# A kernel of window attention and an MLP: the first attention block of a batch moved to the period ahead, loads and casts re-ordered, closing stores on two queues

## The chip, the cores and the metric

The kernel runs on one core of one Trainium2 chip. A core has a matrix engine (TensorE, PE in the profile, its weight loads PEld), a vector engine (VectorE, DVE), a scalar engine (ScalarE, ACT), a general engine (GpSimd, POOL) and a synchronisation engine (SyncE, SP) that here only issues DMAs. Every engine works through its own instruction stream in order and meets the others through semaphores. SBUF is the working memory of 128 partitions, PSUM the memory into which TensorE writes. The metric is the device time of one execution in microseconds. A profile shows one such execution; its span runs from the first to the last instruction.

## The reference

For 8 batches, 8 heads, 576 positions and head width 64, the kernel computes attention in which position i sees the 64 positions i-63 to i, lays the heads side by side (512 columns), and runs a normalised two-layer MLP with a residual:

```python
scores = (1.0 / np.sqrt(D)) * np.matmul(q, k.transpose(0, 1, 3, 2))
mask = (rel >= 0) & (rel < 64)                  # rel = i - j
attn = softmax(np.where(mask, scores, -1e9))
x = np.matmul(attn, v).transpose(0, 2, 1, 3).reshape(B, S, H * D)

xn = (x - mean(x)) / np.sqrt(var(x) + 1e-06) * g_ln
out = x + np.maximum(xn @ w_ch1, 0.0) @ w_ch2   # 512 -> 2048 -> 512
```

All inputs and the output are float32 in HBM; the kernel multiplies in float16 and accumulates in float32.

## The kernel before

**Groups.** The MLP runs on nine groups of 512 rows. Groups 0 to 7 are the first 512 positions of each batch; group 8 gathers the last 64 positions of all eight batches (the tails). A group's rows fall into four blocks of 128 rows. A block of a batch is two windows of 64 queries; a block of group 8 holds the tails of two batches.

**Attention of a block** is cut into steps. `s_mm` forms the scores of a block (16 matmuls L263 into two PSUM tiles `sc`, of which there are two in all) and their exponentials (two ACT operations, L266) into a tile `pt`; `s_mask` multiplies by the mask on DVE (L273). `b_step` multiplies by the values (16 matmuls L291 into `xps`, one PSUM tile in all), divides by the row sums (L294, L297) into the float32 rows `xn`, and takes mean and variance (L299, L302). `z_step` normalises a row block on POOL in four operations (L316 to L319). `zt_step` transposes it on PE (L328), and ACT copies it into `zT` (L331), the input of the MLP.

**Inputs.** `load_qk` and `load_v` fetch a batch's q, k and v from HBM (SP, L92 and L139). The float32 buffers are two per tensor for the halves of q and k and one for v, so a load waits until POOL has cast what was there: `cast_qk` (L126), `cast_v` (L145). `t_main` transposes a half of q or k on PE (L216), and ACT or DVE copies it into `qkT`. Values are kept twice: `vA`, and `vB`, which is `vA` shifted by 64 rows. `make_vB` makes the shift with two DMAs issued by POOL (L163, L164). Tails have the same steps: `load_tail`, `cast_tail` and `t_tail`; their loads use the buffers of q and k.

**MLP of a group.** Sixteen units `l1` (four matmuls of 512 columns, L363, and a ReLU on ACT, L367) are followed, from group 2 on, by fourteen units `stage`: the second layer as seven products of half-sized blocks (L435, eight matmuls of 256 columns a unit), in the order 1, 2, 6, 5, 7, 4, 3, two units each. The sums that these products take as operands come from DVE: `s_sums` (L414) of the hidden values, `w2_sums` (L532) of the weights, once. `post` adds a product into `xn` on DVE (L442); products 1, 6 and 7 share one PSUM tile (`pA`), so product 6 waits for the add of product 1. `store` writes finished rows out (SP, L401); for group 8 `store_rest` does (L395). Groups 0 and 1 have a plain second layer (L375, L499).

**The order of work is written out by hand.** Period g runs the units of group g. After unit i come the steps put into slot i by calls `at(i, step, ...)`; within a slot they run in the order in which the calls were made, and each step appends its instructions to the engines' streams. From period 2 on a period has 30 units (numbers 0 to 29, the first 16 of them `l1`). A slot fixes an order only: a DMA on SP is issued as soon as the ones queued ahead of it are issued and its buffer is free. In period g the attention of batch g+1 is computed and batch g+2 is loaded, cast and transposed. From period 2 on the four blocks of batch g+1 have `s_mm` in slots 1, 5, 10, 15, `b_step` and `z_step` in 6, 11, 16, 21 and `zt_step` in 12, 17, 22, 27. A table places the tail blocks:

```python
TAILS = {3: [0], 5: [1], 7: [2, 3]}
```

The rows `xn` of a batch lie in two buffers of 256 rows out of four, so the rows of batch g+1 overwrite those of batch g-1, once these are stored. The stores of a period are issued after products 4 and 3, which are its last.

## Time and profile before

| What | Value |
|---|---|
| median of 13 runs | 334.2 us (332.93 to 337.15) |
| time of the profiled execution | 335.8 us |
| its span | 334.1 us |
| granted TensorE clock, mean | 0.993 |
| PE busy | 315.2 us, 94% |
| DVE busy | 202.6 us, 61% |
| ACT busy | 174.6 us, 52% |
| POOL busy | 165.0 us, 49% |
| HBM read and written | 38.80 and 9.44 MB |

Times in the profile are microseconds, unless marked ns. A row of a timeline gives the start, the length, the engine, the line and operation, output and inputs, how many instructions were merged, and in brackets how long the engine stood idle before it and what ended that wait. A row of waits gives who waited for what, then the total, the number of times and the longest. A row of busy time by stretch gives the length of the stretch and, for each engine, its busy time and its instructions, then the granted clock (1.00 is full), the share of DMA and its GB/s. Periods 2, 3, 4, 5, 6, 7 and 8 begin at about 98.0, 134.8, 170.9, 203.7, 239.8, 271.2 and 301.9 us. Matmuls overlap in the pipeline, so a busy time of several is longer than the step from one group to the next.

### The profile page before, as it was taken

To read this page: it belongs to the slowest core of one execution; us is meant where nothing else is said; L and a number is where in the kernel's file an instruction comes from. 1 tells how busy PE (TensorE), PEld (TensorE's weight loads), DVE (VectorE), ACT (ScalarE), POOL (GpSimd) and SP (SyncE) were. 2 spreads that over 40 slices of the span, in tenths; PEclk is the share of its full clock that TensorE was granted. 3 is DMA by queue.
4 is the path that set the end of the run, shared out by engine and by line. 5 is a ranking of instruction groups with operands and counts; after the bars stand their busy time and mean duration, and the time that the engine had idled before them with its cause. 6 is when DMAs were issued, how large, how long until landed. Compare 5 with 4: busy or idle time off the path is not lost.

```text
span 334.1 us, 7795 instructions
## 1 busy us (share of the span) xinstructions
PE 315.2 (94%) x3229; PEld 203.9 (61%) x3229; DVE 202.6 (61%) x388; ACT 174.6 (52%) x292; POOL 165.0 (49%) x251
## 2 busy tenths in 40 slices
PE   7998999999996999999899999998999999999992
PEld 4566445786543478546764686466745874685582
DVE  0796583676852796179645964599448744671542
ACT  2486515485356562785357636863477137605600
POOL 7588656503990397448743776377616342420000
PEclk9999999999999899999999999999999999999999
DMA  8999999956129826892059586940391048003013
GB/s 193 290 382 278 343 273 330 264 177 121 65 78 244 191 48 97 238 266 59 3 153 317 108 143 171 301 90 3 76 241 25 0 151 134 2 2 126 0 33 96
DMA packets 85638, 51.08 MB, mean 153 GB/s; under 512 B 55681, under 2 KB 76673, under 8 KB 85602
## 3 DMA queue, kind: packets, MB, share of 16 engines
q1 hardware_dynamic: 84672, 47.98, 53.5%
q0 software_dynamic: 640, 2.33, 3.7%
q8 instruction: 25, 0.41, 0.5%
q10 hardware_dynamic: 290, 0.26, 0.2%
q14 instruction: 11, 0.09, 0.1%
HBM read 38.80 MB, written 9.44 MB: 144 GB/s over the span
## 4 chain that ended last, share of the span: by engine, by line
PE 61%; DMA 11%; DVE 11%; POOL 9%; SPq 3%; issue 3%; ACT 1%; POOLq 0%; ACTq 0%
PE hps L363 22%; PE pA L435 9%; PE pC L435 7%; PE pB L435 6%; PE hph L484 4%; DMA qk<-in_q_dram 4%; DMA w2s<-in_moe_w_ch_dram 3%; DVE sS L414 3%; PE ch L375 3%; PE xps L291 3%; DMA vB<-vA 3%; PE tp L216 3%; PE sc L263 2%; DVE stats L299 2%; DVE xn L297 2%
## 5 line engine op out<-in xcount | busy, mean ns | idle before, releaser
L363 PE MATMUL hps<-zT,w1g 128*128 128x512 f16 x480 | 113.8, 382 | 0.7 <-ACT zT L331 0.7
L367 ACT ACTIVATE hrT<-hps 128x512 f16<-128x512 f32 x120 | 71.9, 601 | 36.9 <-PE hps L363 36.0
L363 PEld LDWEIGHTS <-w1g 128*128 128x128 f16 x480 | 44.0, 98 | 48.7 <-issue 3.5
L316 POOL TENSOR_SCALAR rsz<-mvg 128x1 f32<-128x1 f32 x28 | 12.5, 448 | 90.8 <-DVE mvg L302 90.2
L331 ACT COPY zT<-ztp 128x512 f16<-128x512 f16 x36 | 21.0, 584 | 56.8 <-PE ztp L328 56.7
L435 PEld LDWEIGHTS <-sS 128*128 128x128 f16 x448 | 42.6, 98 | 7.8 <-issue 3.0
L266 ACT ACTIVATE pt<-sc 128x512 f16<-128x512 f32 x72 | 39.0, 597 | 10.5 <-PE sc L263 10.3
L207 ACT COPY qkT<-tp 128x1024 f16<-128x1024 f16 x26 | 26.2, 1012 | 26.5 <-PE tp L216 26.2
L126 POOL CAST qk<-qk 128x1024 f16<-128x1024 f32 x32 | 34.3, 1090 | 8.5 <-DMA qk<-in_q_dram 4.2
L435 PEld LDWEIGHTS <-hrT 128*128 128x128 f16 x336 | 31.7, 98 | 4.1
L273 DVE TENSOR_TENSOR pt<-pt,mask 128x1024 f16<-128x1024 f16 x28 | 19.1, 682 | 23.6 <-ACT pt L266 23.6
L414 DVE TENSOR_TENSOR sS<-hrT 128x512 f16<-128x512 f16 (+1 forms) x42 | 24.7, 588 | 11.1 <-ACT hrT L367 11.1
L442 DVE TENSOR_TENSOR xn<-pA,xn 128x512 f32<-128x512 f32 x28 | 19.2, 685 | 19.0 <-PE pA L435 11.2
L294 DVE RECIPROCAL rcp<-xps 128x8 f32<-128x8 f32 x36 | 7.3, 203 | 38.3 <-PE xps L291 38.1
L435 PE MATMUL pA<-wT,sS 128*128 128x256 f16 x224 | 27.6, 273 | 2.5 <-DVE xn L442 2.5
L435 PE MATMUL pC<-w2s,sS 128*128 128x256 f16 x224 | 27.6, 273 | 0.0
L299 DVE BATCH_NORM_STATS2 stats<-xn 128x6 f32<-128x512 f32 x36 | 25.0, 695 | 1.2
L297 DVE TENSOR_TENSOR xn<-xps,rcp 128x512 f32<-128x512 f32 x36 | 24.9, 691 | 1.2
L319 POOL TENSOR_SCALAR z<-xn,rsz 128x512 f16<-128x512 f32 x28 | 23.9, 852 | 2.9
L484 PE MATMUL hph<-zT,w1g 128*128 128x256 f16 x192 | 23.2, 273 | 1.8 <-ACT zT L331 0.9
L375 PE MATMUL ch<-w2s,hrT 128*128 128x512 f16 x96 | 23.9, 380 | 0.1
L291 PEld LDWEIGHTS <-pt 128*64 128x64 f16 x576 | 12.4, 111 | 15.1 <-issue 10.7
(85 smaller groups left out, 442.4 us busy)
## 6 DMA issues: line engine op xcount, KB each, us to landing
out_dram<-xn SPq DMA_DIRECT2D x34, 256.0 KB, 3.8
qk<-in_q_dram SPq DMA_DIRECT2D x16, 512.0 KB, 7.1
qk<-in_k_dram SPq DMA_DIRECT2D x16, 512.0 KB, 7.7
v<-in_v_dram SPq DMA_DIRECT2D x32, 256.0 KB, 6.1
w2s<-in_moe_w_ch_dram SPq DMA_DIRECT2D x12, 512.0 KB, 5.9
w1s<-in_moe_w_ch_dram SPq DMA_DIRECT2D x4, 512.0 KB, 6.6
tk<-in_k_dram SPq DMA_DIRECT2D x8, 256.0 KB, 4.5
tv<-in_v_dram SPq DMA_DIRECT2D x8, 256.0 KB, 4.7
```

What stands on the lines that cost most here:

```text
L126: nc.gpsimd.tensor_copy(out=dst[:, :].rearrange("p (a j) e d -> p a e j d", j=j), in_=t[:, :].rearrange("p (a e j d) -> p a e j d", e=2, j ...
L207: nc.scalar.copy(out=out, in_=in_)
L266: nc.scalar.activation(out=pt[:, par], in_=sc[par], func=AF.Exp, bias=0.0, scale=scale)
L297: nc.vector.tensor_tensor(out=xn, in0=xps[:, :, 0:D], in1=rcp_b, op=ALU.mult)
L299: nc.vector.bn_stats(out=stats, in_=xv)
L319: nc.gpsimd.tensor_scalar(out=z, in0=xv, scalar1=rs, scalar2=nm, op0=ALU.mult, op1=ALU.add)
L363: nc.tensor.matmul(out=hps, lhsT=w1g[:, kc, 128 * hc:128 * (hc + 1)], rhs=zT[g][:, kc, :], start=(kc == 0), stop=(kc == NKC - 1),)
L367: nc.scalar.activation(out=hrT[:, hc, :], in_=hps, func=AF.Relu, bias=0.0, scale=1.0)
L375: nc.tensor.matmul(out=ch[kb], lhsT=hrT[:, hc, 128 * kb:128 * (kb + 1)], rhs=w2s[:, hc, :], start=(hc == 0), stop=(hc == NHC - 1),)
L414: nc.vector.tensor_tensor(out=o, in0=x, in1=y, op=op)
L435: nc.tensor.matmul(out=bank[which][:, p, :], lhsT=a[:, c, 128 * p:128 * p + 128], rhs=wv[:, c, :], start=(first and p == 0 and c == 0), st ...
L484: nc.tensor.matmul(out=hps[:, e], lhsT=w1g[:, kc, 128 * hc:128 * (hc + 1)], rhs=zT[g][:, kc, 256 * half:256 * half + 256], start=(kc == 0) ...
```

## The change

- Block 0 of a batch has its `s_mm` and `s_mask` in the period ahead (slots 27 and 28; slot 31 in period 1). Blocks 1 to 3 have `s_mm` in 2, 7, 12; `b_step` and `z_step` of all four are in 2, 7, 12, 17, and `zt_step` in 8, 13, 18, 23.
- `load_qk` and `load_v` of batch g+3 are placed in period g, in slots 17, 18 and 23, behind the casts of batch g+2; in period 1 those of batch 4 are added to those of batch 3.
- `cast_qk` of the first half is put ahead of the `b_step` and `z_step` of slot 12 (slot 11, and called earlier than they are), the second in slot 16; `cast_v` and `make_vB` in 20 and 21; `t_main` in 17, 19, 21, 25. In period 1 the same steps come earlier by some six slots.
- Tails have float32 buffers of their own for k and v. Their loads are in slot 5 and their casts in slot 24 of the period ahead, the transpositions (`t_tail`, split in q and k) in 27 and 29; `s_mm` is in slot 1, `b_step` in 5, `zt_step` in 11. The second tail of period 7 is loaded from slot 25 of period 6, cast in slot 3 and transposed in 7 and 8 of period 7, with `s_mm` in 10, `b_step` in 14 and `zt_step` in 20.
- The last two stores go one to SP's queue and one to ACT's, instead of both to ACT's.
- `pt` has four buffers instead of six, and a constant is cut from 128 elements to 1.

```diff
@@ -46,7 +46,7 @@
     p_in = ctx.enter_context(tc.tile_pool(name="pin", bufs=2))
     p_qkt = ctx.enter_context(tc.tile_pool(name="pqkt", bufs=2))
     p_va = ctx.enter_context(tc.tile_pool(name="pva", bufs=2))
-    p_pt = ctx.enter_context(tc.tile_pool(name="ppt", bufs=6))
+    p_pt = ctx.enter_context(tc.tile_pool(name="ppt", bufs=4))
     p_xn = ctx.enter_context(tc.tile_pool(name="pxn", bufs=4))
     p_blk = ctx.enter_context(tc.tile_pool(name="pblk", bufs=3))
     p_grp = ctx.enter_context(tc.tile_pool(name="pgrp", bufs=2))
@@ -96,8 +96,8 @@
 
     def load_tail(i):
         tq = p_in.tile([128, H, D], FP32, tag="tq32", name=f"tq32_{i}", bufs=1)
-        tk = p_in.tile([128, 2, H, D], FP32, tag="qk32_1", name=f"tk32_{i}")
-        tv = p_in.tile([128, 2, H, D], FP32, tag="qk32_0", name=f"tv32_{i}")
+        tk = p_in.tile([128, 2, H, D], FP32, tag="tk32", name=f"tk32_{i}", bufs=1)
+        tv = p_in.tile([128, 2, H, D], FP32, tag="tv32", name=f"tv32_{i}", bufs=1)
         tail32[i] = (tq, tk, tv)
         for r in range(2):
             b = 2 * i + r
@@ -222,20 +222,20 @@
         evac(x if eng is None else eng, dst.rearrange("c h (p j) -> c h p j", j=j),
              tp[:, :].rearrange("c (h j) p -> c h p j", j=j))
 
-    def t_tail(i):
-        q16, k16 = tail16.pop(i)
-        tqk = (p_qkt.tile([128, NHP, 128], FP16, tag="tqT", name=f"tqT_{i}", bufs=1),
-               p_qkt.tile([128, 2, NHP, 128], FP16, tag="tkT", name=f"tkT_{i}", bufs=1))
-        tailT[i] = tqk
-        tp = t_tile([128, 2, NHP, 128], f"tpk_{i}")
-        for r in range(2):
+    def t_tail(i, x):
+        src = tail16[i][x]
+        if x == 0:
+            tailT[i] = (p_qkt.tile([128, NHP, 128], FP16, tag="tqT", name=f"tqT_{i}", bufs=1),
+                        p_qkt.tile([128, 2, NHP, 128], FP16, tag="tkT", name=f"tkT_{i}", bufs=1))
+            tp = t_tile([128, NHP, 128], f"tpq_{i}")
             for hp in range(NHP):
-                nc.tensor.transpose(out=tp[:, r, hp, :], in_=k16[:, r, 2 * hp:2 * hp + 2, :], identity=ident16)
-        evac(0, tqk[1], tp)
-        tp = t_tile([128, NHP, 128], f"tpq_{i}")
-        for hp in range(NHP):
-            nc.tensor.transpose(out=tp[:, hp, :], in_=q16[:, 2 * hp:2 * hp + 2, :], identity=ident16)
-        evac(0, tqk[0], tp)
+                nc.tensor.transpose(out=tp[:, hp, :], in_=src[:, 2 * hp:2 * hp + 2, :], identity=ident16)
+        else:
+            tp = t_tile([128, 2, NHP, 128], f"tpk_{i}")
+            for r in range(2):
+                for hp in range(NHP):
+                    nc.tensor.transpose(out=tp[:, r, hp, :], in_=src[:, r, 2 * hp:2 * hp + 2, :], identity=ident16)
+        evac(0, tailT[i][x], tp)
 
     def s_mm(g, j, pe_mask=False):
         sc = [ps_s.tile([128, NHP, 2, 64], FP32, tag="sc", name=f"sc_{g}_{j}_{par}") for par in range(2)]
@@ -392,7 +392,7 @@
         def store_rest(k0, cols, eng):
             xv = x_norm[(g, k0 // 2)]
             for r in range(2):
-                eng.dma_start(
+                (eng or (nc.sync, nc.scalar)[r]).dma_start(
                     out=out[2 * k0 + r:2 * k0 + r + 3:2, SM:S, cols].rearrange("k s d -> s k d"),
                     in_=xv[64 * r:64 * r + 64, :, cols],
                 )
@@ -471,7 +471,7 @@
                 tbank["shared"] = False
                 tbank["n"] = 0
                 if last:
-                    store_rest(0, slice(256, DM), nc.scalar)
+                    store_rest(0, slice(256, DM), None)
                 else:
                     store(0)
                     store(1)
@@ -535,7 +535,7 @@
     load_qk(0, 0)
     load_v(0, 0, 2)
     g1 = p_const.tile([1, DM], FP32, tag="g1", name="g1")
-    ones1 = p_const.tile([1, 128], FP32, tag="ones1", name="ones1")
+    ones1 = p_const.tile([1, 1], FP32, tag="ones1", name="ones1")
     nc.scalar.dma_start(out=g1, in_=bass.AP(tensor=moe_g_ln.tensor, offset=moe_g_ln.offset, ap=[[DM, 1], [1, DM]]))
     load_qk(0, 1)
     load_v(0, 2, 4)
@@ -691,45 +691,66 @@
                 at(22 + 3 * m, w2_sums, i, 0, 4)
                 at(23 + 3 * m, w2_sums, i, 4, 8)
             for j in range(4):
-                at((9, 13, 16, 20)[j], s_mm, 2, j)
-                at((10, 14, 17, 21)[j], s_mask, 2, j)
-                at((13, 17, 21, 25)[j], b_step, 2, j)
-                at((13, 17, 21, 25)[j], z_step, 2, j)
-                at((19, 23, 27, 31)[j], zt_step, 2, j)
-        if g > 1 and b < B:
-            for j in range(4):
-                at((1, 5, 10, 15)[j], s_mm, b, j)
-                at((2, 6, 11, 16)[j], s_mask, b, j)
-                at((6, 11, 16, 21)[j], b_step, b, j)
-                at((6, 11, 16, 21)[j], z_step, b, j)
-                at((12, 17, 22, 27)[j], zt_step, b, j)
-        for n, i in enumerate(TAILS.get(g, ())):
-            ts = ((3, 5, 6, 9, 15), (14, 16, 17, 20, 26))[n] if g == B - 1 else (3, 8, 9, 13, 19)
-            at(ts[0], t_tail, i)
-            at(ts[1], s_mm, NGRP - 1, i)
-            at(ts[2], s_mask, NGRP - 1, i)
-            at(ts[3], b_step, NGRP - 1, i)
-            at(ts[3], z_step, NGRP - 1, i)
-            at(ts[4], zt_step, NGRP - 1, i)
+                at((9, 13, 16, 19)[j], s_mm, 2, j)
+                at((10, 14, 17, 20)[j], s_mask, 2, j)
+                at((13, 17, 20, 23)[j], b_step, 2, j)
+                at((13, 17, 20, 23)[j], z_step, 2, j)
+                at((19, 23, 26, 30)[j], zt_step, 2, j)
+            at(8, load_qk, 3, 0)
+            at(9, load_qk, 3, 1)
+            at(14, load_v, 3, 0, 4)
+            at(13, alloc_qkT, 3)
+            at(13, cast_qk, 3, 0)
+            at(17, cast_qk, 3, 1)
+            at(21, alloc_v, 3)
+            at(21, cast_v, 3, 0, 2)
+            at(22, cast_v, 3, 2, 4)
+            at(22, alloc_vB, 3)
+            at(22, make_vB, 3)
+            at(31, s_mm, 3, 0)
+            at(31, s_mask, 3, 0)
+            for i, (x, half) in zip((21, 24, 25, 28), ((0, 0), (1, 0), (0, 1), (1, 1))):
+                at(i, t_main, 3, x, half, 0)
+            at(25, load_qk, 4, 0)
+            at(26, load_qk, 4, 1)
+            at(28, load_v, 4, 0, 4)
         if g == 2:
             at(3, w2_sums, 1, 0, 4)
             at(4, w2_sums, 1, 4, 8)
-        if 0 < g and b + 1 < B:
-            n = b + 1
-            e = 20 if g == 1 else 13
-            at(max(e - 12, 2), load_qk, n, 0)
-            at(max(e - 11, 3), load_qk, n, 1)
-            at(e - 6, load_v, n, 0, 4)
-            at(e if g == 1 else e - 1, alloc_qkT, n)
-            at(e if g == 1 else e - 1, cast_qk, n, 0)
-            at(e + 4 if g == 1 else e + 5, cast_qk, n, 1)
-            at(e + 7 if g == 1 else 22, alloc_v, n)
-            at(e + 7 if g == 1 else 22, cast_v, n, 0, 2)
-            at(e + 8 if g == 1 else 23, cast_v, n, 2, 4)
-            at(e + 8 if g == 1 else 23, alloc_vB, n)
-            at(e + 8 if g == 1 else 23, make_vB, n)
-            for (x, half), i in zip(((0, 0), (1, 0), (0, 1), (1, 1)), (24, 26, 28, 30) if g == 1 else (17, 19, 24, 29)):
+        if g > 1 and g + 2 < B:
+            at(11, alloc_qkT, g + 2)
+            at(11, cast_qk, g + 2, 0)
+        if g > 1 and b < B:
+            for j in range(4):
+                if j:
+                    at((2, 7, 12)[j - 1], s_mm, b, j)
+                    at((3, 8, 13)[j - 1], s_mask, b, j)
+                at((2, 7, 12, 17)[j], b_step, b, j)
+                at((2, 7, 12, 17)[j], z_step, b, j)
+                at((8, 13, 18, 23)[j], zt_step, b, j)
+        for n, i in enumerate(TAILS.get(g, ())):
+            ts = (10, 11, 14, 20) if n else (1, 2, 5, 11)
+            at(ts[0], s_mm, NGRP - 1, i)
+            at(ts[1], s_mask, NGRP - 1, i)
+            at(ts[2], b_step, NGRP - 1, i)
+            at(ts[2], z_step, NGRP - 1, i)
+            at(ts[3], zt_step, NGRP - 1, i)
+        n = g + 2
+        if g > 1 and n < B:
+            at(16, cast_qk, n, 1)
+            at(20, alloc_v, n)
+            at(20, cast_v, n, 0, 2)
+            at(21, cast_v, n, 2, 4)
+            at(21, alloc_vB, n)
+            at(21, make_vB, n)
+            for i, (x, half) in zip((17, 19, 21, 25), ((0, 0), (1, 0), (0, 1), (1, 1))):
                 at(i, t_main, n, x, half, 0)
+            at(27, s_mm, n, 0)
+            at(28, s_mask, n, 0)
+            if n + 1 < B:
+                at(17, load_qk, n + 1, 0)
+                at(18, load_qk, n + 1, 1)
+                at(23, load_v, n + 1, 0, 4)
         if g > 1:
             for i in range(1, 5):
                 at(7 + i, s_sums, 0, 4, i)
@@ -737,11 +758,16 @@
                 at((15, 15, 19, 21)[i - 1], s_sums, 6, 8, i)
         for n, i in enumerate(TAILS.get(g + 1, ())):
             if n == 0:
-                at(21, load_tail, i)
-                at(26, cast_tail, i)
+                at(5, load_tail, i)
+                at(24, cast_tail, i)
+                at(27, t_tail, i, 0)
+                at(29, t_tail, i, 1)
+            else:
+                at(25, load_tail, i)
         if len(TAILS.get(g, ())) == 2:
-            at(0, load_tail, TAILS[g][1])
-            at(8, cast_tail, TAILS[g][1])
+            at(3, cast_tail, TAILS[g][1])
+            at(7, t_tail, TAILS[g][1], 0)
+            at(8, t_tail, TAILS[g][1], 1)
         for i, u in enumerate(units):
             if g > 1 and i == 20:
                 tbank["shared"] = True
```

## The prediction

> **What bounds the kernel now.** I read the page first, then busy time by period, then who waited for whom on PE, and last the timelines around each wait.
>
> ```profile
> span 334.1 us, 7795 instructions
> ...
> PE 315.2 (94%) x3229; PEld 203.9 (61%) x3229; DVE 202.6 (61%) x388; ACT 174.6 (52%) x292; POOL 165.0 (49%) x251
> ```
>
> PE works 94% of the span and no other engine more than 61%. The change takes no matrix work away, so only PE's gaps can be won. Busy time cut at the first matmul of periods g = 2, 3 and 4 (stretch, its length, busy us and instructions of each engine, clock, DMA):
>
> ```profile
> core 0: us, PE busy (x) PEld busy (x) DVE busy (x) ACT busy (x) POOL busy (x), PEclk, DMA share, GB/s
> ...
> 98.00:134.80 36.80, 34.06 (x352) 22.18 (x352) 21.57 (x42) 18.41 (x31) 20.84 (x33) 0.95 0.66 144
> 134.80:170.90 36.10, 34.62 (x404) 23.06 (x401) 24.29 (x46) 21.81 (x37) 22.66 (x34) 1.00 0.48 131
> 170.90:203.70 32.80, 32.73 (x355) 21.73 (x353) 20.71 (x41) 19.32 (x32) 18.38 (x29) 1.00 0.76 184
> ```
>
> Period 4 is what an undisturbed period looks like: 32.8 us, PE busy for 32.73. Period 2 has almost the same matmuls (352 against 355) and takes 4.0 us more, part of it at a lower clock. Period 3, with a tail block, has 1.5 us of PE idle. The waits of PE over the whole run (us in total, times, longest):
>
> ```profile
> PE xps L291 <- DMA vB<-vA: 2.6, 1, 2.6
> PE pA L435 <- DVE xn L442: 2.5, 3, 1.1
> ...
> PE ztp L328 <- POOL z L319: 1.3, 3, 0.6
> ```
>
> With one of 0.67 below, these are all the larger ones after the prologue, and all lie at places that the change rearranges: 7.1 us. The prologue's waits are left alone.
>
> **Period 1 into 2.** The PE timeline there:
>
> ```profile
> 96.97 0.39 PE L328 MATMUL ztp<-ident,z 128*128 128x128 f16 x4
> 98.03 1.89 PE L363 MATMUL hps<-zT,w1g 128*128 128x512 f16 x8 [0.67 <-ACT zT L331]
> ...
> 100.19 3.77 PE L363 MATMUL hps<-zT,w1g 128*128 128x512 f16 x16
> ...
> 107.90 0.23 PE L291 MATMUL xps<-vB,pt 128*64 128x65 f16 x1 [2.64 <-DMA vB<-vA]
> ...
> 108.49 4.67 PE L363 MATMUL hps<-zT,w1g 128*128 128x512 f16 x16
> ```
>
> The last transposition of batch 2 ends the period, and the next layer needs its copy at once: 0.67. Then block 0 of batch 3 waits 2.64 for the shifted values, and the 16 matmuls behind it take 4.67 where 3.77 is usual: 0.90 lost to the clock. Each break costs a little beyond its idle time, because matmuls overlap. The size of that comes from a break in period 6 (timeline), beside the same 16 matmuls unbroken on the chain of waits:
>
> ```profile
> 259.20 1.91 PE L435 MATMUL pB<-w2s,hrT 128*128 128x256 f16 x16
> 261.43 1.80 PE L435 MATMUL pA<-wT,sS 128*128 128x256 f16 x15 [0.32 <-DVE xn L442]
> ```
> ```profile
> 166.90 1.75 PE pB L435 x16
> ```
>
> The step is 2.23 where 1.75 is usual: 0.48, of which 0.32 is shown as idle, so 0.16 a break. The boundary loses 0.67 + 2.64 + 2 x 0.16 + 0.90 = 4.5 us.
>
> After the change block 0's scores go to period 1's end (slot 31), its values are wanted at slot 2 instead of 6, and the shift of V is issued at slot 22 instead of 28. What sets the issue is POOL's queue:
>
> ```profile
> 85.42 0.32 POOL L203 MEMSET qkT<- 128x256 f16 x1
> 85.68 2.02 POOL L126 CAST qk<-qk 128x1024 f16<-128x1024 f32 x2
> ...
> 90.26 1.09 POOL L319 TENSOR_SCALAR z<-xn,rsz 128x512 f16<-128x512 f32 x1
> ...
> 93.40 0.51 POOL L316 TENSOR_SCALAR rsz<-mvg 128x1 f32<-128x1 f32 x1
> ...
> 95.87 0.76 POOL L319 TENSOR_SCALAR z<-xn,rsz 128x512 f16<-128x512 f32 x1
> ...
> 99.08 0.74 POOL L163 DMA_DIRECT2D vB<-vA  x1
> 99.83 0.54 POOL L164 DMA_DIRECT2D vB<-vA  x1
> ```
>
> From 85.42 to 100.37 POOL has no gap worth the name. The first half's cast (0.3 + 2.0) moves ahead into an earlier gap, so this block of 15.0 us shrinks to about 12.7 and would end at 98.1; but its order is now: second cast, z of block 2, cast of V, shift of V, and only then z of block 3. That z therefore ends between 97 (if its parts run at their quick times) and 98.1; I take 97.4. PE comes to its transposition, now in slot 30, at about 96.1, which is when today's slot 31 begins (96.97 less the 0.87 of a unit, half of the 1.75 above). A new wait of 1.3 (bounds 0.9 to 2.0) stands where 0.67 stood. The copy to zT is then covered by one unit and the scores moved there.
>
> The shift is issued ahead of that z (3.2 long today, 93.40 to 96.63) and takes 1.3 to issue, so at about 93. Its landing, min, median and max, first copy:
>
> ```profile
> DMA to landing us min/median/max: 3.4/3.5/8.7
> ```
>
> The 8.7 is this boundary's, with loads of Q and K on the queues; they are there after the change as well, so I keep 8.7: 101.7. PE wants it at 97.5 + 0.2 + 0.9 + 0.35 (to the period's start; scores take 0.41 less overlap, below) + three units and one set of scores (3.0), about 101.9. That is too close to call: I put 0.2; bounds 0 (landing in 3.5) and 2 (issue a microsecond later and the landing a microsecond slower). Short breaks of 1.12 stand in a stretch of full clock (period 3 above), so the 0.90 goes too. The boundary keeps 1.5 of 4.5: **3.0 won**, between 1.0 and 4.5.
>
> Against 97.4 speaks the Trainium skill, "SBUF — State Buffer", section "Who interferes with whom": a VectorE operation with two inputs in SBUF and a GpSimd one that reads SBUF shut each other out for a whole instruction. The weight sums of slots 22 to 29 are of that kind and would stand beside the moved z of block 3, whose upper bound, a wait of 2.0, would then hold: 2.3 won instead of 3.0. The trace agrees half way: z took 1.09 at 90.26, amid such sums, and 0.76 at 95.87 where they were over.
>
> **Tail periods 3 and 5.** In period 3 (PE, then DVE) a wait of pA and one of ztp (this belongs to the tail's z, queued behind the casts of slot 12):
>
> ```profile
> 158.38 0.40 PE L328 MATMUL ztp<-ident,z 128*128 128x128 f16 x4 [0.36 <-POOL z L319]
> ...
> 160.34 1.91 PE L435 MATMUL pA<-wT,sS 128*128 128x256 f16 x16 [1.12 <-DVE xn L442]
> ```
> ```profile
> 159.61 0.68 DVE L442 TENSOR_TENSOR xn<-pA,xn 128x512 f32<-128x512 f32 x1
> ```
>
> The product needs the add of L442, which stood on DVE behind slot 16's block step and mask. After the change that step is in slot 17, issued behind the add, the masks are at 13 or earlier and the tail's step at 5. Both waits go: 0.36 + 1.12 + 2 x 0.16 = 1.8 a period. The one of period 6 (0.48) goes the same way, and the 0.59 + 0.16 of period 7, where the last tail's cast, now at slot 3, is still held by the buffer of V until slot 5, but its transpositions come at 7 and 8 and its z at 14.
>
> New is that the tail's scores (slot 1) and block 1's (slot 2) are one unit apart, with two score buffers in all. A pair of exponentials beside its scores, PE and then ACT:
>
> ```profile
> 144.73 0.41 PE L263 MATMUL sc<-tqT,tkT 64*128 64x64 f16 x16
> ```
> ```profile
> 145.32 1.08 ACT L266 ACTIVATE pt<-sc 128x512 f16<-128x512 f32 x2
> ```
>
> They end (146.40) 1.67 after the scores began; the next scores come 0.34 + 0.87 after, and wait 0.46, so 0.5 (bounds 0 and 1.0, if ACT is still at the tail's key copy). Periods 3 and 5 win 2 x (1.8 - 0.5) = **2.6**; periods 6 and 7 **1.2**.
>
> **Loads and buffers.** Loads of a later batch wait for the casts that free their buffers (slots 11, 16, 21), so they fall to the second half of a period, when now only stores are queued; SP's stores stand behind them. Cost taken as nothing: loads have a period of cover, and the shift of V, issued and wanted earlier by about as much, keeps its lead (the first rival prices the doubt). Fewer exponential buffers (4) cost nothing, as at most three blocks are live. But block 0 now writes its rows at slot 2, into the buffer that the last stores of the period before read. Landing of the stores at the end of period 3 and of period 7:
>
> ```profile
> DMA to landing us min/median/max: 3.8/5.8/6.0
> ```
> ```profile
> DMA to landing us min/median/max: 2.0/2.1/2.3
> ```
>
> The first share the queues with loads that follow them, the second are alone. After the change no load follows them, so I take near 2 and a cost of nothing; 5.8 is a rival below.
>
> **The end.** SP's own last issue, then the closing pair on ACT, with the pair's issue times:
>
> ```profile
> 328.06 0.60 SPq L395 DMA_DIRECT2D out_dram<-xn  x1
> 328.72 1.70 ACTq L395 DMA_DIRECT2D out_dram<-xn  x2
> ```
> ```profile
> L395 ACTq DMA_DIRECT2D out_dram<-xn x2: 636/674/712, 328.7 to 329.8; - x2
> ```
>
> The second starts 1.1 after the first and could start with it on SP, free at 328.66. Between 0 (SP's larger stores in front) and 1.1: **0.5**.
>
> **Sum.** 3.0 + 2.6 + 1.2 + 0.5 = 7.3. Against the profiled execution's 335.8 (span 334.1 and 1.7 around it) that is 328.5; against the median of the runs, 334.2, it is 326.9. The profiled one is slower by 1.6, which may or may not sit in waits that I count: 327.5 between the two.
>
> **Rivals.** *Waits come back half* (0.20): the shift of V lands late at more boundaries. In period 4 it is issued late today (timeline of POOL):
>
> ```profile
> 202.25 0.59 POOL L163 DMA_DIRECT2D vB<-vA  x1
> ```
>
> That is 31.3 into the period; four units, two sets of transpositions and one of scores earlier make it about 26, right behind the V loads. With 8.7 it lands at 34.7 and is wanted at 35.8 (32.8 + 3.0). The slack of 1.1 speaks against; for it that every such issue now meets loads. At 10.5 it costs about 0.7 at four boundaries, and with z of block 3 at its upper bound 0.7 more: 7.3 - 3.5 = 3.8 won, 330.5.
>
> *Nothing moves* (0.12): the waits were only where a backlog of DVE or ACT surfaced, and it surfaces at the next product. Against it: DVE is busy 20.71 of 32.8 in period 4 and PE idles under 0.1 there. Then only the end and a little of the boundary remain: 333.5.
>
> *Closing stores in the way* (0.10, the slower side): the stores land at 5.8 as at period 3 now. Issued about 1.3 into the next period, they free the buffer at 7.1, and block 0's write on DVE was due at 3.6. What follows it, in period 4 now (PE; then POOL):
>
> ```profile
> 178.45 3.63 PE L363 MATMUL hps<-zT,w1g 128*128 128x512 f16 x16
> ...
> 184.57 0.39 PE L328 MATMUL ztp<-ident,z 128*128 128x128 f16 x4
> ```
> ```profile
> 183.10 0.76 POOL L319 TENSOR_SCALAR z<-xn,rsz 128x512 f16<-128x512 f32 x1
> ```
>
> z is done at 183.86 for 184.57, a slack of 0.7, so periods 4 and 6 wait 3.5 - 0.7 = 2.8 each; in 3 and 5, due 1.3 later, the tail's mask stands behind the write on DVE and the tail's values wait 2.2 each. 10.0 lost against 7.3 won: 336.9 on the median. It turns the sign from a landing of about 5.1 and is told from no change from 5.5.
>
> **Chances and range.** The forecast has 0.58, for 324.5 to 329.7. A measurement tells about 0.5%, 1.7 us, from no change. The forecast, the half return and a sliver of the rest are faster: 0.80; nothing moves is mostly the same: 0.09; slower 0.11. The range runs from 323.5 (every counted wait gone, 4.5 + 3.6 + 1.2 + 1.1) to 332.5, the half return with a margin.
>
> **What would show it.** PE in period 2 without a wait above 1 us before xps and a clock of 1.00; pA without a wait for DVE; a wait of about 1.3 before the last ztp of period 1; about 0.5 before the second scores in periods 3 and 5; periods 3 and 5 near 34.8 long. I am wrong if xn of L297 waits for stores, if xps waits for vB in periods 3 to 6, or if products wait for DVE elsewhere.

## The result and the profile after

| What | Before | After |
|---|---|---|
| median of the runs | 334.84 us (332.93 to 338.5) | 325.05 us (324.31 to 325.59) |
| time of the profiled execution | 335.8 us | 325.05 us |
| its span | 334.1 us | 323.3 us |

Before's median is now over all of its runs, not over the 13 shown ahead. The ratio of the times is 0.9701, with a 95% interval of 0.967 to 0.9732: the changed kernel is faster by 3.0%. The forecast was 327.5 us, from 323.5 to 332.5. The direction and the range held, and the gain was larger than the sum: 10.8 us of span against 7.3.

The head of the page after:

```profile
span 323.3 us, 7813 instructions
...
PE 310.5 (96%) x3229; PEld 204.7 (63%) x3229; DVE 203.0 (63%) x388; ACT 176.8 (55%) x292; POOL 163.6 (51%) x251
```

The matmuls are the same 3229, and the busy times of the other engines change by about 2 us at most. Busy time by stretch, cut at the first matmul of each period: of before, the periods 1 and 5 to 8 (2, 3 and 4 stand in the prediction), then of after all eight.

```profile
59.36:98.00 38.64, 37.25 (x425) 25.90 (x424) 28.18 (x61) 22.73 (x36) 19.31 (x30) 1.00 0.49 135
...
203.70:239.80 36.10, 34.63 (x404) 23.05 (x402) 24.29 (x46) 21.80 (x37) 22.67 (x34) 1.00 0.47 131
239.80:271.20 31.40, 31.09 (x325) 20.05 (x323) 20.61 (x40) 16.29 (x29) 12.73 (x20) 1.00 0.39 89
271.20:301.90 30.70, 30.11 (x274) 19.83 (x272) 16.43 (x30) 15.19 (x26) 7.75 (x12) 1.00 0.35 78
301.90:334.10 32.20, 26.06 (x176) 17.00 (x174) 11.75 (x21) 9.55 (x16) 0.00 (x0) 0.98 0.22 66
```
```profile
59.10:99.50 40.40, 37.77 (x441) 26.21 (x439) 29.72 (x61) 22.62 (x36) 22.62 (x35) 1.00 0.70 201
99.50:132.35 32.85, 32.85 (x370) 22.66 (x365) 23.47 (x44) 21.26 (x35) 20.94 (x31) 1.00 0.85 186
132.35:165.65 33.30, 33.30 (x392) 22.70 (x389) 23.13 (x45) 21.99 (x36) 20.10 (x31) 1.00 0.53 141
165.65:198.50 32.85, 32.85 (x367) 22.66 (x366) 21.93 (x42) 20.23 (x33) 20.61 (x31) 1.00 0.76 186
198.50:231.80 33.30, 33.30 (x391) 22.68 (x389) 23.06 (x45) 21.99 (x36) 20.10 (x31) 1.00 0.20 57
231.80:262.40 30.60, 30.60 (x318) 20.65 (x317) 20.64 (x41) 15.20 (x27) 12.72 (x20) 1.00 0.45 110
262.40:291.60 29.20, 29.20 (x264) 19.25 (x261) 15.61 (x30) 14.47 (x25) 7.27 (x12) 1.00 0.15 49
291.60:323.30 31.70, 26.25 (x178) 17.12 (x176) 11.75 (x21) 9.55 (x16) 0.00 (x0) 0.98 0.23 67
```

Periods 2 to 7 of after have no idle PE left (PE's busy time equals the stretch). To compare period with period, the work that the change moves has to be taken out: a set of scores with the change of form around it takes 0.45, and a tail's transpositions take 0.68 (0.23 for q and 0.45 for k, from one start to the next in the PE timeline of after). What was moved into a period is added to its gain, and what was moved out is taken off.

| Place | shorter by | moved work | gain | forecast |
|---|---|---|---|---|
| periods 1 and 2 (the boundary) | -1.76 + 3.95 | 0.45 + 0.68 | 3.3 | 3.0 |
| periods 3 and 5 (tails) | 2.80 each | -0.68 each | 4.2 | 2.6 |
| period 4 | -0.05 | 0.68 | 0.6 | 0 |
| periods 6 and 7 | 0.80 + 1.50 | 0.68 - 0.45 - 0.68 | 1.85 | 1.2 |
| period 8 and the end | 0.50 | | 0.5 | 0.5 |
| prologue | 0.26 | | 0.3 | 0 |

The parts add up to the 10.8 of span, but for rounding. What was named ahead as a sign stands in the waits of PE in after (in us: total, times, longest):

```profile
PE ztp L328 <- POOL z L319: 1.4, 1, 1.4
...
PE hph L484 <- DVE xn L385: 0.5, 1, 0.5
```

The wait of xps for vB and those of pA for DVE are gone. The wait of ztp is the one forecast at the end of period 1. That of `hph` is at the start of period 1; what is left out lies in the prologue and periods 0 and 1 too.

### The profile page after: what moved, and what is told of

Read it like the earlier page. It is cut to its first block, busy times and chain, and to the rows that moved or that the text cites. A ratio compares the mean times of both kernels' runs of the same rounds, so it can differ in the third digit from the quotient of the medians.

```text
span 323.3 us, 7813 instructions
## 1 busy us (share of the span) xinstructions
PE 310.5 (96%) x3229; PEld 204.7 (63%) x3229; DVE 203.0 (63%) x388; ACT 176.8 (55%) x292; POOL 163.6 (51%) x251
## 4 chain that ended last, share of the span: by engine, by line
PE 81%; POOL 5%; DVE 4%; SPq 4%; DMA 2%; issue 1%; ACT 1%; POOLq 0%; ACTq 0%
PE hps L363 33%; PE pA L435 11%; PE pC L435 8%; PE pB L435 8%; PE hph L484 6%; PE tp L216 3%; PE xps L291 3%; PE sc L263 3%; PE ch L375 3%; DMA w1s<-in_moe_w_ch_dram 2%; PE ztp L328 2%; SPq L139 2%; SPq L87 1%; DVE z L312 1%; POOL w1g L188 1%
## 5 line engine op out<-in xcount | busy, mean ns | idle before, releaser
L363 PE MATMUL hps<-zT,w1g 128*128 128x512 f16 x480 | 112.0, 380 | 0.0
L363 PEld LDWEIGHTS <-w1g 128*128 128x128 f16 x480 | 44.1, 98 | 46.9 <-issue 1.0
L266 ACT ACTIVATE pt<-sc 128x512 f16<-128x512 f32 x72 | 39.0, 595 | 15.6 <-PE sc L263 14.1
L126 POOL CAST qk<-qk 128x1024 f16<-128x1024 f32 x32 | 33.4, 1059 | 10.8 <-DMA qk<-in_q_dram 7.4
L414 DVE TENSOR_TENSOR sS<-hrT 128x512 f16<-128x512 f16 (+1 forms) x42 | 21.4, 509 | 10.2 <-ACT hrT L367 10.2
L435 PE MATMUL pA<-wT,sS 128*128 128x256 f16 x224 | 26.9, 273 | 0.0
L435 PE MATMUL pC<-w2s,sS 128*128 128x256 f16 x224 | 26.8, 273 | 0.0
L273 DVE TENSOR_TENSOR pt<-pt,mask 128x1024 f16<-128x1024 f16 x28 | 21.1, 761 | 8.6 <-ACT pt L266 8.6
L297 DVE TENSOR_TENSOR xn<-xps,rcp 128x512 f32<-128x512 f32 x36 | 24.9, 691 | 2.5 <-DMA out_dram<-xn 1.4
L319 POOL TENSOR_SCALAR z<-xn,rsz 128x512 f16<-128x512 f32 x28 | 23.3, 833 | 2.9
L484 PEld LDWEIGHTS <-w1g 128*128 128x128 f16 x192 | 18.2, 98 | 5.6 <-issue 2.7
```

Source lines behind the costliest of these rows:

```text
L126: nc.gpsimd.tensor_copy(out=dst[:, :].rearrange("p (a j) e d -> p a e j d", j=j), in_=t[:, :].rearrange("p (a e j d) -> p a e j d", e=2, j ...
L266: nc.scalar.activation(out=pt[:, par], in_=sc[par], func=AF.Exp, bias=0.0, scale=scale)
L297: nc.vector.tensor_tensor(out=xn, in0=xps[:, :, 0:D], in1=rcp_b, op=ALU.mult)
L319: nc.gpsimd.tensor_scalar(out=z, in0=xv, scalar1=rs, scalar2=nm, op0=ALU.mult, op1=ALU.add)
L363: nc.tensor.matmul(out=hps, lhsT=w1g[:, kc, 128 * hc:128 * (hc + 1)], rhs=zT[g][:, kc, :], start=(kc == 0), stop=(kc == NKC - 1),)
L414: nc.vector.tensor_tensor(out=o, in0=x, in1=y, op=op)
```

## The experiments

The explanation to be tested: the gain comes from where the steps stand against the work queued on POOL and DVE (the early shift of V at the first boundary; the block step behind the product's add; the casts ahead of the normalised row). Against it stood these: that it comes from block 0's scores being a period ahead; that it comes from buffers or queues; that a single reorder would do; and, on the slower side, that loads ahead of stores decide. Short names: "the cast" is `cast_qk` of the first half.

### One queue for the closing stores (from after)

```diff
-                    store_rest(0, slice(256, DM), None)
+                    store_rest(0, slice(256, DM), nc.scalar)
```

> The changed kernel, with both closing stores on ACT's queue again. If the second queue is what shortened the end (from the last matmul's start to the span's end 6.4 us before, 5.7 after), the time is 0.3 to 0.9 us longer than the changed kernel's 325.05, and ACT's second issue starts about 1.1 us behind its first. If the end is set by the transfers alone, the time is the same within 0.3.

Measured: 324.69 us (324.05 to 325.39), ratio 0.9688 (0.9643 to 0.9734): as after. The second queue brings nothing. From the last matmul's start to the span's end after takes 5.75 us, this kernel 5.63, and before 6.36, so the end is shorter for another reason (see the buffers, below). The Trainium skill, "DMA: Bandwidth & Descriptors", section "Issuing engines are not separate DMA queues", says that issuing from several engines saves the issue time alone; the run agrees, and here not even that issue time reached the end.

### Block 1's scores ahead of block 0's values (from after)

```diff
         if g > 1 and b < B:
+            at(2, s_mm, b, 1)
```

Block 1's own call in the loop, in slot 2, is dropped.

> The changed kernel, with the scores of block 1 put ahead of block 0's values inside slot 2, the order that the prediction took for granted. If the 0.5 us that it counted for two sets of scores close together was right and was only hidden by the 16 value matmuls standing between them, PE now waits about 0.5 us for the exponentials in periods 3 and 5, and the time grows by about 0.9 (0.6 to 1.3). If ACT is quick enough anyway, no wait shows and the time is the same within 0.3.

Measured: 325.95 us, ratio 0.972 (0.9669 to 0.9771), which the times don't tell from after; the trace does. The start of period 3 on PE, first in after, then in this kernel:

```profile
134.18 0.41 PE L263 MATMUL sc<-tqT,tkT 64*128 64x64 f16 x16
134.52 1.04 PE L363 MATMUL hps<-zT,w1g 128*128 128x512 f16 x4
135.48 0.22 PE L291 MATMUL xps<-vB,pt 128*64 128x65 f16 x1
...
135.87 0.43 PE L263 MATMUL sc<-qkT,qkT 64*128 64x64 f16 x16
```
```profile
134.74 0.41 PE L263 MATMUL sc<-tqT,tkT 64*128 64x64 f16 x16
...
136.05 0.20 PE L263 MATMUL sc<-qkT,qkT 64*128 64x64 f16 x1
136.47 0.39 PE L263 MATMUL sc<-qkT,qkT 64*128 64x64 f16 x15 [0.22 <-ACT pt L266]
```

In after the tail's exponentials end at 135.86 (the ACT row is `134.78 1.08 ACT L266 ACTIVATE pt<-sc 128x512 f16<-128x512 f32 x2`), and PE reaches block 1's scores at 135.87, because block 0's 16 value matmuls stand between the two sets. With the scores first the wait is there, and periods 3 and 5 take 33.69 instead of 33.30. So the 0.5 a period that the prediction charged is real work of ACT, but the order within the slot hides it to a hundredth of a microsecond.

### The cast behind the normalised row (from after)

```diff
-            at(11, alloc_qkT, g + 2)
-            at(11, cast_qk, g + 2, 0)
...
+            at(12, alloc_qkT, n)
+            at(12, cast_qk, n, 0)
```

The new calls come after those of `b_step` and `z_step`.

> The changed kernel, with the first cast of q and k behind the normalised row of slot 12 again (the second part of the change undone). If the order on POOL matters, the cast ends behind the z of block 2 and the first transposition in slot 17 waits for it: about 0.4 us in periods 2 and 4, about 1.2 in periods 3 and 5, so 2 to 4 us more than the changed kernel, with waits of PE on POOL's cast at L216. If POOL has slack enough there, the time is the same within 0.5.

Measured: 330.37 us (329.0 to 330.75), ratio 0.9853 (0.9806 to 0.99): 5.3 us slower than after, about half of the whole gain. Its largest new wait of PE:

```profile
PE tp L216 <- POOL qk L126: 3.6, 4, 0.9
```

POOL casts after the four operations of the row instead of before them, so the transposition of the cast tile waits 0.9 in four periods; in period 4 the values of a block wait another 0.9 for their mask. Periods 2 to 5 take 33.82, 34.28, 35.09 and 34.31. Of the edits of the change that were undone or made alone here, this one moves the time most.

### Casts and shift of period 1 still earlier; closing stores cut in two (from after)

```diff
-            at(13, cast_qk, 3, 0)
-            at(17, cast_qk, 3, 1)
-            at(21, cast_v, 3, 0, 2)
-            at(22, cast_v, 3, 2, 4)
-            at(22, make_vB, 3)
+            at(10, cast_qk, 3, 0)
+            at(11, cast_qk, 3, 1)
+            at(15, cast_v, 3, 0, 2)
+            at(15, cast_v, 3, 2, 4)
+            at(18, make_vB, 3)
```

> The changed kernel, with batch 3's casts in period 1 moved into the 10 us in which POOL stands idle before its first z: the casts of q and k to slots 10 and 11, those of V to 15, the shift of V to 18. If POOL's queue order is what makes the last transposition of period 1 wait (1.37 idle and 0.16 of overlap), that wait goes and the time falls by 1.2 to 1.6, to about 323.6. If loads or the clash with DVE set it, a wait of 0.5 or more stays there and the time falls by less than 1.

Measured: 324.27 us (323.45 to 324.59), ratio 0.9675 (0.963 to 0.972). The wait of ztp, 1.4 in after, is gone, but span and median fall by only 0.8. A new wait stands in its place, and the DVE timeline shows why; first after at the same place, then this kernel and its wait of PE:

```profile
70.86 3.07 DVE L209 CAST vB<-v 64x512 f16<-64x512 f32 x7
```
```profile
70.79 5.38 DVE L209 CAST vB<-v 64x512 f16<-64x512 f32 x7
76.20 0.69 DVE L273 TENSOR_TENSOR pt<-pt,mask 128x1024 f16<-128x1024 f16 x1
```
```profile
PE xps L291 <- DVE pt L273: 0.8, 1, 0.8
```

The same seven copies take 5.38 us instead of 3.07. In after POOL is idle until 78.64; here it casts q and k from 69.27 to 74.55 (the last two of four):

```profile
72.07 2.48 POOL L126 CAST qk<-qk 128x1024 f16<-128x1024 f32 x2 [0.31 <-DMA qk<-in_q_dram]
```

The mask behind the copies is late, and the values behind the mask. The Trainium skill, "SBUF — State Buffer", section "Who interferes with whom", says that a cast of VectorE in its two-port mode and a GpSimd instruction block each other for a whole instruction; the slower copies and the two last casts (1.24 each where 1.04 is usual) agree with it. Whether these copies run in that mode isn't shown by any run.

The next kernel adds the stores to this: the right half of the columns of row blocks 2 and 3 is stored after product 7 instead of together with the left half after product 4, and all closing stores of group 8 alternate between SP and ACT.

```diff
                 post("A", 2, 0)
+                if last:
+                    store_rest(2, slice(256, DM), None)
...
-                    store_rest(2, slice(0, DM), nc.sync)
+                    store_rest(2, slice(0, 256), None)
...
-                    store_rest(0, slice(0, 256), nc.sync)
+                    store_rest(0, slice(0, 256), None)
```

> The run with batch 3's casts early, and the closing stores of the last group cut so that columns 256 to 511 of its second half leave one product earlier, with all of the group's stores split over SP's and ACT's queues. If the end is set by the bytes still to be stored when the last add is done, it shortens by another 0.3 to 1.0 us. If it is set by the latency of one store, it stays the same within 0.3.

Measured: 323.12 us (321.87 to 323.99), ratio 0.9611 (0.958 to 0.9642); its slowest run lies below after's fastest (324.31). The end shrinks from 5.75 to 4.90 us. The third kernel of this line also moves two of the eight DVE copies behind the mask, and `newton` from slot 13 to 15:

```diff
-            for c in range(4):
+            for c in range(3):
                 at(7, vB_cur, 2, c, 1)
-                if c < 3:
+                if c < 2:
                     at(7, vB_prev, 2, c, 1)
...
+            at(10, vB_cur, 2, 3, 1)
+            at(10, vB_prev, 2, 2, 1)
```

> The run with early casts and cut closing stores, and in period 1 two of DVE's seven copies for the shift of batch 2's V put behind the mask of block 0, the Newton step for batch 1 behind block 0's step. In the run with early casts these copies, beside POOL's casts, made the mask late and PE waited 0.94 for it. If DVE's queue order is what is left of that, the wait goes and the time falls by 0.7 to 1.0 from 323.1, to about 322.3. If the clash slows the mask itself, 0.5 or more of the wait stays.

Measured: 323.02 us (322.1 to 323.87), ratio 0.9617 (0.9576 to 0.9657): not told from the one before. The wait for the mask shrinks from 0.8 to 0.5, at another place, and waits of the first group's second layer for its weights come to 1.8 (0.2 in after), so the difference of 0.3 is lost among them. Both kernels beat both the kernel before and the changed one, by about 12 and 2 us.

### The block step one slot later, alone (from before)

```diff
-                at((6, 11, 16, 21)[j], b_step, b, j)
-                at((6, 11, 16, 21)[j], z_step, b, j)
-                at((12, 17, 22, 27)[j], zt_step, b, j)
+                at((6, 11, 17, 21)[j], b_step, b, j)
+                at((6, 11, 17, 21)[j], z_step, b, j)
+                at((12, 17, 23, 27)[j], zt_step, b, j)
```

> The kernel before, with one edit: the block step of slot 16 is put into slot 17, behind the add that product 6 waits for (its transposition from 22 to 23). If the order on DVE alone causes the waits of pA in periods 3, 5 and 6 (1.28, 1.28 and 0.48 with overlap), they go without anything being brought forward, and the time falls by 2.5 to 3.1 us. If they only show a backlog of DVE, a wait of that size appears at the next product or transposition and the time falls by less than 1.

Measured: 335.04 us, ratio 0.9963 (0.9934 to 0.9992), a span shorter by 0.8. Its waits of PE:

```profile
PE xps L291 <- DMA vB<-vA: 2.8, 1, 2.8
PE ztp L328 <- POOL z L319: 2.4, 3, 0.9
...
PE tp L216 <- POOL qk L126: 1.4, 2, 0.7
```

The waits of pA for DVE, 2.5 in before, are gone: the block step was their cause. But the wait of ztp grows from 1.3 to 2.4, and transpositions wait for the cast, 1.4. With the old order on POOL the backlog only surfaces one engine further. The 0.8 of span also holds two things that the edit didn't make: the prologue and period 1 took 1.0 longer than in before (period 2 begins at 99.03), and the 16 matmuls behind the wait for vB ran at their usual length, where they took 4.67 in before:

```profile
109.48 3.63 PE L363 MATMUL hps<-zT,w1g 128*128 128x512 f16 x16
```

The rival "nothing moves" was nearly right for this edit by itself; the whole change escapes it by moving the cast too.

### The shift of V early, alone (from before)

```diff
-            at(e if g == 1 else e - 1, cast_qk, n, 0)
-            at(e + 4 if g == 1 else e + 5, cast_qk, n, 1)
+            at(13 if g == 1 else e - 1, cast_qk, n, 0)
+            at(17 if g == 1 else e + 5, cast_qk, n, 1)
...
-            at(e + 8 if g == 1 else 23, make_vB, n)
+            at(22 if g == 1 else 23, make_vB, n)
```

The other steps of period 1 move as in the change (the casts of V to 21 and 22, the transpositions, batch 2's blocks); block 0 stays in its own period.

> The kernel before, with one edit: period 1 has the changed kernel's slots for batch 3's casts, transpositions and shift of V and for batch 2's steps, but block 0 stays in period 2 with its values wanted at slot 6. If the late shift of V causes the wait of 2.64 and the low clock behind it, both go (3.7 with overlap), while the last transposition waits about 0.7 longer than before, as in the changed kernel: the time falls by 2.5 to 3.5. If the clock falls for another cause, it stays near 0.95 in period 2 and the time falls by 2 at most.

Measured: 333.09 us (332.11 to 334.06), ratio 0.9915 (0.9882 to 0.9949). Periods 1 and 2 by stretch, and one of its waits of PE:

```profile
59.00:98.10 39.10, 36.98 (x424) 25.75 (x422) 28.28 (x59) 22.64 (x36) 21.61 (x34) 1.00 0.54 147
98.10:131.10 33.00, 32.93 (x353) 21.72 (x352) 22.25 (x43) 18.42 (x31) 18.41 (x29) 1.00 0.63 147
```
```profile
PE pA L435 <- DVE xn L442: 2.6, 3, 1.1
```

The wait for vB is gone, the clock stays at 1.00 and period 2 takes 33.0 instead of 36.8; the tails' waits stay. Periods 1 and 2 together take 72.1 instead of 75.4, which is the 3.3 of the whole change. The boundary is therefore won by the earlier steps of period 1, the shift of V among them, without block 0 ahead, and the two causes are separate.

### Half of the loads between the closing stores (from after)

```diff
-                at(18, load_qk, n + 1, 1)
+                at(28, load_qk, n + 1, 1)
```

> The changed kernel, with the second half of the loads of q and k in periods 2, 3 and 4 moved from slot 18 to 28, between the two pairs of closing stores. This is the price of the slower rival. If block 0's rows wait for the buffer that the last stores read, each of three period starts has these stores land about 3.4 us later (1 MB at some 300 GB/s), DVE's wait at L297 grows from 0.2 to 0.7 to some 4, and PE waits about 3 in periods 3 and 5 and 2.3 in period 4: 6 to 9 us slower than the changed kernel. If slack covers it, the time is the same within 1.

Measured: 324.91 us (324.75 to 325.16), ratio 0.9668 (0.9641 to 0.9695): as after. The stores of a period (L401, issue to landing) go from a median of 4.2 in after, at the end of period 3, to 6.0, and DVE waits longer for them; first after, then this kernel:

```profile
DVE xn L297 <- DMA out_dram<-xn: 1.4, 3, 0.7
```
```profile
DVE xn L297 <- DMA out_dram<-xn: 2.1, 3, 1.2
```

PE waits for none of it. The rows of block 0 go into the buffer that the first pair of stores reads (after product 4), not the last pair, so these loads stood behind the stores that matter.

### All loads of q and k ahead of all closing stores (from after)

```diff
-                at(17, load_qk, n + 1, 0)
-                at(18, load_qk, n + 1, 1)
+                at(25, load_qk, n + 1, 0)
+                at(26, load_qk, n + 1, 1)
```

> The changed kernel, with all loads of q and k in periods 2, 3 and 4 moved from slots 17 and 18 to 25 and 26, behind those of V and ahead of all four closing stores. The run with late loads had put them behind the first pair of stores, and the instruction order shows that block 0's rows go into the buffer which that first pair reads, not the last pair as the prediction said. If stores queue behind loads, 3 MB of loads from about 26 us into a period end near 38, the first pair lands 5 to 6 us into the next period, DVE's wait at L297 grows from 0.2 to 0.7 to 2.5 to 4, and PE waits 1.5 to 3 in periods 3, 4 and 5, for a mask or a z: 4 to 9 us slower than the changed kernel. If stores are served beside the loads, DVE's wait stays under 1.5 and the time is the same within 1.

Measured: 351.02 us (349.63 to 352.18), ratio 1.0461 (1.0405 to 1.0517): 16 us slower than before and 26 slower than after. Its waits of PE, its wait of L297 on DVE, and the landing of the stores at the end of a period:

```profile
PE xps L291 <- POOL rsz L316: 14.9, 2, 8.4
PE xps L291 <- DVE pt L273: 5.6, 1, 5.6
```
```profile
DVE xn L297 <- DMA out_dram<-xn: 23.9, 3, 9.0
```
```profile
DMA to landing us min/median/max: 8.1/8.3/8.3
```

And the issue of the stores by SP at the end of period 2, first in after, then in this kernel:

```profile
130.52 4.12 SPq L401 DMA_DIRECT2D out_dram<-xn  x4
```
```profile
134.45 2.30 SPq L401 DMA_DIRECT2D out_dram<-xn  x4
```

The mechanism of the slower rival exists: block 0's rows wait for the buffer, the mask and the next blocks wait behind them on DVE, and PE behind those. (The view puts 14.9 down to POOL's rsz; in period 3 that operation ends within 0.1 us of the mask, which the values need.) It was underpriced, though: 10.0 lost in the prediction, 26 measured. The rows were ready at 130.4 in after and at 130.6 here, but here the stores stand behind the loads in SP's queue until 134.45, and only then come the 8.3: block 0's write runs at 143.5, where it was due at 136.4 (it waited 7.0). The clock, 1.00 in periods 2 to 7 of after, is 0.97 over this run.

### The buffers alone (from before)

```diff
-        tk = p_in.tile([128, 2, H, D], FP32, tag="qk32_1", name=f"tk32_{i}")
-        tv = p_in.tile([128, 2, H, D], FP32, tag="qk32_0", name=f"tv32_{i}")
+        tk = p_in.tile([128, 2, H, D], FP32, tag="tk32", name=f"tk32_{i}", bufs=1)
+        tv = p_in.tile([128, 2, H, D], FP32, tag="tv32", name=f"tv32_{i}", bufs=1)
```

The four `pt` buffers and the smaller constant come with it.

> The kernel before with the changed buffers alone: tails' k and v with buffers of their own, four buffers instead of six for the exponentials, the short constant; no step moves. From the last matmul's start to the end of the span the kernel before takes 6.36 us, the changed one 5.75, and 5.63 with both closing stores on one queue again, so the queue is not the cause. If the place of the rows in SBUF is, the end here is 5.6 to 5.8 as well and the time falls by about 0.6. If the cause lies in the order of the work, the end stays at 6.4. No wait of PE in the middle should change under either (below 0.3 us).

Measured: 335.69 us, ratio 1.0013 (0.9979 to 1.0047): no change in time. But its end takes 5.63 us, as in the kernel with one queue, against 6.36 in before. Landing of the tails' stores (L395), first in before, then in this kernel:

```profile
DMA to landing us min/median/max: 2.4/3.2/4.2
```
```profile
DMA to landing us min/median/max: 2.5/3.0/3.6
```

The slowest store lands 0.6 sooner, though nothing about stores was edited; only what lies where in SBUF differs. The other traces bear this out: the slowest takes 4.3 and 4.2 in the two other kernels with before's buffers, and 3.6 to 3.9 in those with the changed buffers and after's or before's stores. Why that matters to them wasn't settled.

### Block 0 in its own period (from after)

```diff
-            at(31, s_mm, 3, 0)
-            at(31, s_mask, 3, 0)
...
+            at(0, s_mm, b, 0)
+            at(0, s_mask, b, 0)
...
-            at(27, s_mm, n, 0)
-            at(28, s_mask, n, 0)
```

> The changed kernel, with block 0's scores and mask in slot 0 of its own period instead of slots 27 and 28 of the period ahead; all else stays, so its values are wanted at slot 2. If the move to the period ahead is needed for the early steps, PE waits in each of periods 2 to 6 for the mask (exponentials 1.67 after the scores, the mask 0.7 and a release, against two units of 1.74): 0.6 to 1.0 each, and in periods 3 and 5 the tail's scores one unit behind add up to 0.5: 4 to 6 us slower. If the slack of the early steps is enough without it, the time is the same within 0.5.

Measured: 326.41 us (326.07 to 327.77), ratio 0.9726 (0.9682 to 0.977), 1.4 us above after. Its waits of PE that after doesn't have:

```profile
PE xps L291 <- DVE pt L273: 0.8, 3, 0.3
...
PE sc L263 <- ACT pt L266: 0.6, 2, 0.3
```

With block 0's scores in slot 0 the values come before their mask (periods 2, 4 and 6), and the tail's scores before ACT is free (3 and 5). That is all that the period ahead is worth once the other steps are in place: 1.4 of some 10 us, so the edit named first in the change brings only a small share of it.

## Why the prediction was right, and where its terms were off

**The boundary of periods 1 and 2 (3.0 forecast, 3.3 measured).** The wait that takes the place of the old ones is where it was put, and its size: PE and POOL in after,

```profile
97.98 0.40 PE L328 MATMUL ztp<-ident,z 128*128 128x128 f16 x4 [1.37 <-POOL z L319]
```
```profile
94.01 0.74 POOL L163 DMA_DIRECT2D vB<-vA  x1
...
97.16 0.76 POOL L319 TENSOR_SCALAR z<-xn,rsz 128x512 f16<-128x512 f32 x1
```

1.37 against 1.3; z ends at 97.92, between the 97 and 98.1 of the bounds. The shift was issued at 94.0, a microsecond later than worked out (93), but its first copy landed after 6.5 us, not 8.7 (3.0 to 6.5 over the run), at 100.5 for values that PE began at 102.25: the term of 0.2 was 0. The clock's loss came back, with 1.00 in period 2, also in the kernel with the early shift alone, and it was larger than the 0.90 counted: from the start of the values to the next scores before takes 5.19, and the kernels with the later block step and with the early shift take 3.94, so 1.25. Another 0.5 went to a wait of `hph` at the start of period 1, which has no counterpart in before.

The stronger reading of the Trainium skill's "SBUF — State Buffer", section "Who interferes with whom", by which the wait would be 2.0, was not put to the test here. The last weight sums on DVE ended at 96.00, before z L319 began at 97.16, and its 0.76 is its quick time:

```profile
94.72 1.28 DVE L532 TENSOR_TENSOR wT<-w2s,wT 128x1024 f16<-128x1024 f16 x2
```

**Tail periods (2.6 forecast, 4.2 measured): the step that failed.** Both waits went, as said, 1.8 a period. The term "the tail's scores (slot 1) and block 1's (slot 2) are one unit apart ... so 0.5" was wrong: the count of what stands between them left out block 0's value matmuls, which the same slot queues first. 134.52 to 135.87 is 1.35, not 0.87. Putting the scores first brought the wait back (33.69 against 33.30). That pA waited for the block step of slot 16 is shown by the kernel in which that step alone moves; the earlier slots of the tails' own steps were not tried alone.

The remaining 0.3 a period, and most of the 0.6 in period 4, were not counted at all. They lie in changes of the matmul's form. In period 4 of before, the same four matmuls of L363 ahead of value matmuls and ahead of a transposition:

```profile
182.35 1.04 PE L363 MATMUL hps<-zT,w1g 128*128 128x512 f16 x4
183.32 0.22 PE L291 MATMUL xps<-vB,pt 128*64 128x65 f16 x1
...
183.70 1.04 PE L363 MATMUL hps<-zT,w1g 128*128 128x512 f16 x4
184.57 0.39 PE L328 MATMUL ztp<-ident,z 128*128 128x128 f16 x4
```

The first step takes 0.97, the second 0.87: going over to the narrow form costs 0.1. Before, scores and values stood in different slots, so that cost came twice a block; after, the next block's scores follow the values directly in three slots a period. So 3 x 0.1 is worked out; no run tested it alone. In period 4 a step of 0.45 instead of 0.23 between a ztp and the tp behind it is gone as well. The length named as a sign, 34.8 for periods 3 and 5, was missed by 1.5: 0.5 for that term, 0.3 for the forms, and 0.68 because the transpositions that move into the period ahead were not taken off. Periods 6 and 7 gained 1.85 where 1.2 was forecast; the forms, worked out as above, are worth 0.3 of that in period 6, and the rest stays open.

**The order of the casts.** The prediction put its worth into the block of POOL at the boundary and into the tails' ztp waits. The kernel with the cast behind the row shows that periods 2 to 5 rest on it: 5.3 us without it, a price that can't be added to the others, as the edits lean on each other. The forecast was right to price both edits together, since the block step alone gave only 0.8 of span.

**Loads and buffers (0 forecast, 0 measured, but for another reason).** "The buffer that the last stores of the period before read" was the wrong buffer; it is that of the first pair. L297 does wait for those stores (1.4 in three, 0.7 at most), which the prediction had named as a sign of being wrong. It costs nothing because the next deadline is further off: in period 4 of after, DVE, POOL and PE,

```profile
169.79 0.69 DVE L297 TENSOR_TENSOR xn<-xps,rcp 128x512 f32<-128x512 f32 x1 [0.72 <-DMA out_dram<-xn]
```
```profile
173.16 0.76 POOL L319 TENSOR_SCALAR z<-xn,rsz 128x512 f16<-128x512 f32 x1
```
```profile
175.11 0.39 PE L328 MATMUL ztp<-ident,z 128*128 128x128 f16 x4
```

z is done at 173.92 for 175.11, a slack of 1.2. "Near 2" for the stores' landing was wrong too: the medians are 5.1, 4.2 and 3.4 at the ends of periods 2 to 4. The rival named "closing stores in the way" was therefore a real danger, held off by loads that are queued in slots 17 and 18, ahead of the stores by many units; queued at 25 and 26 they make the kernel slower than before.

**The end (0.5 forecast, 0.5 measured): right size, wrong cause.** It isn't the second queue (the kernel with one queue has the same end) but the shorter landing that comes with the changed buffers, to which the prediction gave no worth. That the two sizes agree is luck.

**The basis.** From the profiled execution the sum gave 328.5, from the median 326.9, and the forecast lay between. From the profiled execution's 335.8 the measured 10.8 gives 325.0, which is the profiled time of after. The error of 2.5 us is thus that of the sum (10.8 less 7.3 is 3.5), less the 1.0 that the middle had already given away. The rivals' times (330.5, 333.5 and 336.9) were worked out from the median 334.2 alone, so they stand 0.8 lower against the forecast than its own basis would put them.

## What to carry to other kernels

A step that is moved should be followed past everything that its own slot queues ahead of it, because a dozen short matmuls between two sets of scores decided here whether ACT's 1.08 us showed. Taking away a wait by one reorder may only hand the backlog to the next engine (DVE to POOL here), so the queue behind it has to be reordered in the same edit. When loads move, look at which stores free the buffer that is written first, and at what stands ahead of those stores in the issuing queue, not at their landing times.

## What was not expected of the hardware

- The clock loss after the wait for vB varies from run to run. In the profiled executions of before, of before with the changed buffers and of before with the later block step, PE waited 2.64, 2.82 and 2.84 us there, and the 16 matmuls L363 behind the values took 4.67, 5.31 and 3.63: much the same wait cost 1.0, 1.7 and nothing. Among the eleven runs of before that stood beside the kernel with all loads ahead, the mean granted clock was 0.985 to 0.990 in the five that took 336.4 to 338.2 us, and 0.994 to 0.999 in the six that took 333.5 to 335.3; on another chip the two go together less closely (0.993 at 337.0). With the shift early (333.09 us) the spread is 2.0 us, in after 1.3. A wait of 2.6 to 2.8 us can be enough for that loss, and isn't always. The Trainium skill, "TensorE: Matmul & The Clock Gate", section "What's actually happening", gives an idle window of about 3.4 us for it; here the wait was shorter than that.
- Going over from four matmuls of L363 to narrow ones costs PE 0.1 us (0.97 where 0.87 is the step to a transposition), with no idle time shown.
- The placement of buffers in SBUF changed the slowest closing store by 0.6 us (4.2 to 3.6), with the same instructions around it, and the other traces fall on the two sides alike. The cause is open.
- Loads queued ahead of stores cost 26 us, while loads queued behind the stores that free the buffer cost nothing, although their stores land 1.8 us later.
